# Two normalisations on VectorE, and batch 2's k turned ahead of its last two loads, in a fused windowed attention and MLP kernel

## The chip, the cores and the metric

The kernel runs on one core of one Trainium2 chip. A core has TensorE (PE: matmuls, with weight loads listed as PEld), VectorE (DVE), ScalarE (ACT), GpSimd (POOL) and SyncE (SP), each with its own in-order queue of instructions, and DMA queues that the engines feed. The metric is the device time of one execution in microseconds (us), the median over several runs. A profile, which lists every instruction of one further execution, explains it.

## The reference

Causal attention with a window of 64 keys over 8 batches, 8 heads, 576 positions and 64 columns per head; its output, as 4608 rows of 512, goes through two matrix products with h * cos(h) between them.

```python
scores = scale * np.matmul(q, k.transpose(0, 1, 3, 2))
rel = pos[:, None] - pos[None, :]
mask = (rel >= 0) & (rel < window)
scores = np.where(mask, scores, -1000000000.0)
attn = softmax(scores)                       # over the last axis
x = np.matmul(attn, v).transpose(0, 2, 1, 3).reshape(4608, 512)
h = x @ w_in                                 # 512 x 2048
out = (h * np.cos(h)) @ w_out                # 2048 x 512
```

## The kernel before, in words

**Units, groups, tiles.** Heads are taken in four pairs, and the 576 positions in nine blocks of 64, so a batch has 36 units (pair, block) of 128 partitions by 128 keys. A *group* is three or four units that go through the softmax together. The output rows are cut in nine M-tiles of 512 rows; M-tile `mt` covers eight blocks, so tile 1 holds the last block of batch 0 and blocks 0 to 6 of batch 1, tile 2 holds blocks 7 and 8 of batch 1 and blocks 0 to 5 of batch 2, and so on.

**The path of a group.** `g_scores` or `burst` multiplies q and k on TensorE (`s_ps`, L240 or L257). `g_max` adds the mask and takes the maximum on VectorE (`s`, `negm`, L273). `g_exp` takes exponentials and their sums on ScalarE (`e`, `den`, L284). `g_inv` inverts the sums on VectorE (`rden`, L291). `g_norm` multiplies e by rden into `w` on GpSimd (L298), unless it is given another engine. `g_trans` turns w: by TensorE into PSUM (`tw_ps`, L307) with a copy by `g_put` (L108) for the groups named in `direct`, otherwise by a DMA transpose from SP into `wT` (L310). `values` multiplies wT and v on TensorE (`o_ps`, L326), `put_x` copies that to `xT`, and the two products follow: `h_ps` (L347), sine on ScalarE (L489), product on VectorE (`gT`, L492), `out_ps` (L504), a copy to `out_sb` and a store.

**Where q and k come from.** Batches 0 and 1 are loaded whole and turned by TensorE. From batch 2 on `load_chunk` (L148, issued by GpSimd) brings q and k in five chunks of 128 positions each (the fifth has 64) into a row tile. Even and odd batches do not use different row tiles: batch 1 has `rows1`, all others share `rows0`. Slots 0 to 4 of the row tile hold the five q chunks and k's fifth chunk, slots 5 to 8 hold k's chunks 0 to 3. Two DMA transposes from SP (`turn`, L152) then make the turned tile `T`: `turn(b, 0, 5)`, called the q turn below, and `turn(b, 5, 9)`, the k turn. `load_v` (L158) brings v, also in five chunks from GpSimd, and `spread_v` copies its halves so that each block finds its 128 keys.

**The order.** The order on each engine is that of the program: tile 0 follows a list written out by hand (`FIRST`), and everything else is put on a plan with `at(time, function, ...)`. The matmul loops of an M-tile call `pump(time)`, which calls all planned steps up to that time in order of time. One M-tile takes `T = 32` units of planned time. The planned times only order the steps; the engines then run as their waits allow. A step that reads what a transfer writes waits for that transfer if the transfer was called earlier. If the reader is called first, the transfer waits for the reader.

**Before, around the change.** Batch 2's k chunks 0 to 3 are planned at 27.5, 28.4, 29.3 and 30.2, its k turn at 39.2 (7.2 into tile 1's time), behind all of them. Batch 3's k chunks are planned from 47 on. `g_norm` of batch 1's groups runs on GpSimd. The first of these groups is the last block of batch 0, the second is block 6 of batch 1. Tile 0's two stores are planned at 40 and 41, behind the k turn on SP.

**Resources that bind neighbours.** GpSimd's loads use eight completion counters in turn, so a load waits until the load eight places earlier has landed. Each SP transfer uses eight counters likewise. `w` has eight buffers, `e` six, `out_sb` three.

Of the kernel before, what the change touches and what calls it, by code (L numbers as in the profile page):

```python
# [33 lines left out]
T = 2 * Q  # L34
# [17 lines left out]
def kernel(  # L52
# [49 lines left out]
    def bank(which, name):  # L102
        if which == "t":
            return ps_t.tile([128, 512], F32, tag="t", name=name)
        return ps.tile([128, 512], F32, tag=which, name=name)

    def copy(engine, out, in_):
        {"a": nc.scalar.copy, "p": nc.gpsimd.tensor_copy}.get(engine, nc.vector.tensor_copy)(out, in_)  # L108
# [229 lines left out]
    def exp_table():  # L338
        nc.scalar.activation(small, small, AF.Exp, scale=0.0)
# [4 lines left out]
    def first(mt, ff, ks, start, stop):  # L344
        if start:
            st["h", ff] = bank((H_BANKS if mt else H_FIRST)[ff], "h_ps")
        nc.tensor.matmul(out=st["h", ff], lhsT=w_in_sb[:, ks, ff * 128:ff * 128 + 128],  # L347
                         rhs=st["xT", mt][:, ks], start=start, stop=stop)

    def skewed(mt, ks, n):  # L350
        for ff in range(SKEW):
            first(mt, ff, ks, n == 0, n == PAIRS - 1)

    def last_rows(gT, o_sb):
        ms = MT // 128 - 1
        for which, lo, hi in (("O1", 0, LAST), ("S", LAST, d_model)):
            o_ps = bank(which, "out_ps")[:, lo:hi]
            for ff in range(n_ff):
                nc.tensor.matmul(out=o_ps, lhsT=gT[ff // 2][:, ff % 2, ms * 128:ms * 128 + 128],  # L359
                                 rhs=w_out_sb[:, ff, lo:hi], start=ff == 0, stop=ff == n_ff - 1)  # L360
            to = moe.tile([128, MT], F32, tag="sin", name="last_sb", bufs=4)[:, lo:hi] if lo else o_sb[:, 1, lo:hi]
            copy("d" if lo else "a", to, o_ps)
            (nc.sync if lo else nc.scalar).dma_start(out=out[n_mt * MT - 128:n_mt * MT, lo:hi], in_=to)

    def store(o_sb, mt, ms0, e, n):
        r0 = mt * MT + (ms0 + e) * 128
        nc.sync.dma_start(out=out[r0:r0 + n * 128].rearrange("(a p) f -> p a f", p=128), in_=o_sb[:, e:e + n])
# [3 lines left out]
    def at(time, fn, *args):  # L371
        plan.append((time, len(plan), fn, args))

    def pump(time):
        plan.sort(key=lambda x: x[:2])
        while plan and plan[0][0] <= time:
            _, _, fn, args = plan.pop(0)
            fn(*args)
# [3 lines left out]
    n = n_first  # L382
    for t in range(B - 1):
        last = max(i for i, units in enumerate(groups) if units[0][0] == t + 1)
        time = T * t + Q - 1.4
        times = [time]
        for i in range(n, last + 1):
            times.append(times[-1] + PACE * len(groups[i]))
        if t:
            at(times[0], burst, n, BURSTS[0])  # L390
            at(times[4] + 0.1, burst, n + 4, BURSTS[1])
        else:
            for i in range(0, last + 1 - n, 2):
                at(times[max(i - 1, 0)] + (0.5 if i else 0), burst, n + i, (S_BANKS[i % 3], S_BANKS[(i + 1) % 3]))
        for i in range(last + 1 - n):
            time = times[i] + (0.3 if i > 3 and t else 0)
            lags = LAGS[:2] + tuple(T * t + T - 0.79 - time + 0.01 * s for s in range(3)) if n == last and t else LAGS
            for lag, fn in zip(lags, (g_max, g_exp, g_inv, g_norm)):
                at(time + lag, fn, n)
            at(time + (4.6 if n in direct else lags[-1]) if not t or i < 6 else T * t + T + 0.1 * i, g_trans, n)  # L400
            if n in direct:
                at(time + 4.9, g_put, n)
            ready.update({unit: time + (5.9 if n in direct else 8.5) for unit in groups[n]})
            n += 1
# [5 lines left out]
    for b in range(2, B):  # L410
        t0 = T * (b - 1)
        for c in range(NC):
            at(t0 - T + (4 + 0.5 * c if b == 2 else 5 + 0.9 * c), load_chunk, "q", b, c)
            at(t0 - T + ((27.5 if b == 2 else 15 if b == 3 else 10.5) + 0.9 * c if c < 4 else 6.5 if b == 2 else 9.6),
               load_chunk, "k", b, c)
            at(t0 + (0.5 if b == 2 else 14) + 0.8 * c, load_v, b, c)
        at(t0 - (4.1 if b == 2 else 5.6), turn, b, 0, 5)
        at(t0 + (7.2 if b == 2 else -5.5), turn, b, 5, 9)
        for half in range(2):
            at(t0 + 27.5 + half, spread_v, b, half, "d")  # L420
    for half in range(2):
        at(17.5, spread_v, 1, half, "dma")
    for mt in range(1, n_mt):
        for p in range(PAIRS):
            time = max(ready[b, p - p % 2 + i // TU, j] for i in range(2 * TU) for b, j in (divmod(mt * TU + i % TU, NU),))
            time = max(time, 25.5) if mt == 1 else T * mt - (8.01 if mt == n_mt - 1 else 1.01)
# [43 lines left out]
    for mt in range(n_mt):  # L470
        base = mt * T
        gT = []
        if mt:
            for ks in range(PAIRS):
                pump(max([base - 1] + [time for time, _, fn, args in plan
                                       if fn is put_x and args[:2] == (mt, ks)
                                       or mt == 1 and fn is values and args == (mt, ks + 1)]))
                skewed(mt, ks, ks)
        for ff in range(n_ff):
            for ks in range(PAIRS):  # L480
                if ff >= SKEW:
                    first(mt, ff, ks, ks == 0, ks == PAIRS - 1)
            h_ps = st.pop(("h", ff))
            sin = moe.tile([128, MT], F32, tag="sin", name="sin", bufs=4)
            if ff % 2 == 0:
                gt = moe.tile([128, 2, MT], BF16, tag="gT", name="gT", bufs=n_ff // 2 + 2)
                gT.append(gt)
            e = ff % 2
            nc.scalar.activation(sin, h_ps, AF.Sin, bias=math.pi / 2.0)  # L489
            if ff == n_ff - 1 and mt < B - 1:  # L490
                exp_table()
            nc.vector.tensor_tensor(out=gt[:, e], in0=h_ps, in1=sin, op=ALU.mult)  # L492
            pump(base + ff)
        half = n_ff // 2 if mt == 0 else n_ff
        for ms0 in range(0, MT // 128, 2):
            o_sb = moe.tile([128, 2, d_model], F32, tag="out", name="out_sb", bufs=3)
            o_ps = [bank(which, "out_ps") for which in (("O0",) if mt == n_mt - 1 and ms0 else ("O0", "O1"))]
            for step, (lo, e) in enumerate([(lo, e) for lo in range(0, n_ff, half) for e in range(2)]):
                ms = ms0 + e
                if mt == n_mt - 1 and ms == MT // 128 - 1:  # L500
                    last_rows(gT, o_sb)
                    break
                for ff in range(lo, lo + half):
                    nc.tensor.matmul(out=o_ps[e], lhsT=gT[ff // 2][:, ff % 2, ms * 128:ms * 128 + 128],  # L504
                                     rhs=w_out_sb[:, ff], start=ff == 0, stop=ff == n_ff - 1)
                    if ff % 4 == 3:
                        if ff == n_ff - 1:
                            copy("a" if e else "d", o_sb[:, e], o_ps[e])
                            if mt == n_mt - 1:
                                store(o_sb, mt, ms0, e, 1)  # L510
                        pump(base + Q + 4 * ms0 + step * half // 4 + ff % half // 4)
            if mt < n_mt - 1:
                at(base + T + (1.5 if mt else 8) + ms0 / 2, store, o_sb, mt, ms0, 0, 2)


# [28 lines left out]
```

## Time and profile before

| | us |
|---|---|
| median of 3 runs | 311.0 |
| lowest, highest | 310.4, 311.55 |
| profiled execution, its own time | 313.43 |
| its span, first to last instruction | 311.7 |

The span is what the profile's rows add up to; times in the rows count from its start. A row of the timeline gives the start, the duration, the engine, the line of the code, the operation with its output and input tiles, how many such instructions were merged, and in brackets how long the engine had been idle and who released it. Rows that end in DMA issues (`POOL ... DMA_DIRECT2D`, `SPq ...`) are the issuing only; when the data has landed is given apart. "PE s_ps <- DMA T" in brackets means that TensorE's matmul into `s_ps` stood until the transfer into `T` had landed. In the table by stages, the column after the engines is the granted TensorE clock (1.00 is full), then the DMA share and GB/s.

### The profile page before, as it was taken

What the parts mean: (1) busy time and instruction counts of PE and PEld (TensorE: products, weight loads), DVE (VectorE), ACT (ScalarE), POOL (GpSimd) and SP (SyncE); (2) the same over time, 40 slices, a digit from 0 to 9 for tenths busy, and PEclk for the clock granted to TensorE, in tenths of its full rate; (3) what the DMA queues carried; (4) which work ended last, traced back from release to release, by engine and by line L of the source; (5) the groups of instructions that cost most, each with busy time, mean ns of one, the idle gap of its engine ahead of it and who ended that gap; (6) DMA issues with size and microseconds to landing.
All of it is one profiled execution on the core that took longest, in us unless ns stands there. A gap on an engine that the chain in (4) does not pass through costs nothing.

```text
span 311.7 us, 7846 instructions
## 1 busy us (share of the span) xinstructions
PE 290.8 (93%) x2628; PEld 143.2 (46%) x2668; DVE 217.3 (70%) x831; ACT 236.2 (76%) x785; POOL 174.2 (56%) x202
## 2 busy tenths in 40 slices
PE   3769998898899999999999999999999999999995
PEld 2635444443345444544454445444544454454443
DVE  2875887668467887788778877887788878335701
ACT  4888689777798789978996999699969986116600
POOL 8996247894564976497649775967902630000000
PEclk9998999999799999999999999999999999999999
DMA  6999999899969999899999998999993342011011
GB/s 90 164 211 207 208 161 109 98 165 165 231 96 147 141 234 149 131 149 233 161 136 148 230 157 156 142 229 145 138 195 114 76 111 92 0 70 68 0 67 69
DMA packets 165577, 43.58 MB, mean 140 GB/s; under 512 B 154720, under 2 KB 161056, under 8 KB 165536
## 3 DMA queue, kind: packets, MB, share of 16 engines
q0 software_dynamic: 99632, 18.36, 74.9%
q1 hardware_dynamic: 65760, 24.52, 39.4%
q8 instruction: 21, 0.34, 0.4%
q10 hardware_dynamic: 144, 0.20, 0.2%
q14 instruction: 20, 0.16, 0.2%
HBM read 36.70 MB, written 9.44 MB: 148 GB/s over the span
## 4 chain that ended last, share of the span: by engine, by line
PE 76%; ACT 6%; DMA 6%; DVE 4%; POOL 4%; issue 3%; DVEq 0%; POOLq 0%; SPq 0%; ACTq 0%
PE h_ps L347 36%; PE out_ps L504 32%; ACT e L284 5%; DMA T<-rows 3%; PE o_ps L326 3%; PE s_ps L257 3%; DMA rows<-in_k_dram 2%; DVE s L273 2%; POOL w L298 1%; PE out_ps L359 1%; DMA rows<-in_q_dram 1%; DVE negm L269 1%; PE tw_ps L307 1%; POOL v L108 1%; POOL rows L148 1%
## 5 line engine op out<-in xcount | busy, mean ns | idle before, releaser
L347 PE MATMUL h_ps<-xT,w_in 128*128 128x512 bf16 x556 | 127.0, 381 | 2.2 <-DVE xT L108 0.6
L504 PE MATMUL out_ps<-w_out,gT 128*128 128x512 bf16 x543 | 124.5, 383 | 2.0 <-issue 1.3
L492 DVE TENSOR_TENSOR gT<-h_ps,sin 128x512 bf16<-128x512 f32 x144 | 95.6, 689 | 35.3 <-ACT sin L489 35.1
L489 ACT ACTIVATE sin<-h_ps 128x512 f32<-128x512 f32 x144 | 83.1, 599 | 34.2 <-PE h_ps L347 33.3
L284 ACT ACTIVATE e<-s,negm 128x128 f32<-128x128 f32 x256 | 98.7, 388 | 3.3 <-DVE negm L273 3.1
L298 POOL TENSOR_TENSOR w<-e,rden 128x512 bf16<-128x512 f32 (+1 forms) x78 | 77.1, 1001 | 39.1 <-DVE rden L291 35.2
L347 PEld LDWEIGHTS <-w_in 128*128 128x128 bf16 x576 | 56.1, 98 | 66.7 <-issue 1.8
L504 PEld LDWEIGHTS <-gT 128*128 128x128 bf16 x560 | 53.5, 98 | 63.7 <-issue 2.4
L273 DVE CUSTOM_DVE_ANT_0 s<-s_ps,mask 128x128 f32<-128x128 f32 x256 | 58.0, 284 | 2.2 <-PE s_ps L257 2.2
L284 ACT ACTIVATION_READ_ACCUMULATOR e<-s,negm 128x1 f32 x256 | 48.1, 188 | 0.0
L158 POOL DMA_DIRECT2D v<-in_v_dram x40 | 34.0, 876 | 11.0 <-PE out_ps L504 5.2
L148 POOL DMA_DIRECT2D rows<-in_q_dram x30 | 25.5, 872 | 22.1 <-DMA T<-rows 12.7
L108 ACT COPY out_sb<-out_ps 128x512 f32<-128x512 f32 (+1 forms) x18 | 10.2, 566 | 25.4 <-PE out_ps L504 19.9
L148 POOL DMA_DIRECT2D rows<-in_k_dram x30 | 25.7, 897 | 5.5 <-DMA T<-rows 5.5
L291 DVE RECIPROCAL rden<-den 128x4 f32<-128x4 f32 (+1 forms) x80 | 13.7, 172 | 16.6 <-ACT e L284 15.8
L108 DVE COPY out_sb<-out_ps 128x512 f32<-128x512 f32 x18 | 12.4, 689 | 17.0 <-PE out_ps L504 17.0
L108 DVE CAST xT<-o_ps 128x512 bf16<-128x512 f32 x27 | 17.5, 678 | 6.1 <-PE o_ps L326 5.8
L273 DVE DVE_READ_ACCUMULATOR2_ANT negm<- 128x1 f32 x256 | 21.2, 83 | 0.0
L257 PE MATMUL s_ps<-T 64*64 64x128 bf16 x512 | 11.8, 220 | 2.2 <-DMA T<-rows 2.2
L284 ACT ACTIVATE e<-s_ps,negm 128x128 f32<-128x128 f32 x32 | 11.4, 415 | 2.2 <-DVE negm L269 2.2
L257 PEld LDWEIGHTS <-T 64*64 64x64 bf16 x512 | 8.1, 106 | 10.4 <-issue 5.7
L326 PEld LDWEIGHTS <-v 128*64 128x64 bf16 x576 | 10.6, 112 | 4.7 <-issue 2.5
(50 smaller groups left out, 137.2 us busy)
## 6 DMA issues: line engine op xcount, KB each, us to landing
out_dram<-out_sb SPq DMA_DIRECT2D x16, 512.0 KB, 6.1
v<-in_v_dram POOLq DMA_DIRECT2D x32, 128.0 KB, 8.5
rows<-in_q_dram POOLq DMA_DIRECT2D x24, 128.0 KB, 5.8
rows<-in_k_dram POOLq DMA_DIRECT2D x24, 128.0 KB, 8.2
w_out<-in_moe_w_out_dram POOLq DMA_DIRECT2D x2, 1024.0 KB, 16.9
w_in<-in_moe_w_in_dram POOLq DMA_DIRECT2D x2, 768.0 KB, 12.7
wT<-w SPq DMA_TRANSPOSE x66, 3.7
out_dram<-out_sb SPq DMA_DIRECT2D x3, 256.0 KB, 2.0
```

The lines of the kernel that those rows point to most:

```text
L108: {"a": nc.scalar.copy, "p": nc.gpsimd.tensor_copy}.get(engine, nc.vector.tensor_copy)(out, in_)
L148: nc.gpsimd.dma_start(out=rows(b)[lo:lo + n, slot * 512:slot * 512 + 512].rearrange("p (h d) -> p h d", h=H), in_={"q": q, "k": k}[name][b ...
L158: nc.gpsimd.dma_start(out=vt.rearrange("p (h d) -> p h d", h=H), in_=v[b, :, c * 128:c * 128 + n, :].rearrange("h p d -> p h d"))
L257: nc.tensor.matmul(out=s_ps[cross][to, u].rearrange("p (a t) -> p a t", a=2), lhsT=q_cols(b, p, j)[d], rhs=k_cols(b, p, j)[d], start=True, ...
L273: nc.vector.tensor_tensor_reduce(out=s[:, u], in0=s_ps[:, u], in1=mask[:, 2 - j % 2 if j else 0], scale=-scale if b else -1.0, scalar=BIG, ...
L284: nc.scalar.activation(e[:, u], s[:, u], AF.Exp, bias=negm[:, u:u + 1], scale=1.0 if n < n_first else -1.0, accum_out=den[:, u:u + 1])
L298: (nc.gpsimd if engine == "p" else nc.vector).tensor_tensor(out=w[:, 0:u], in0=e[:, 0:u], op=ALU.mult, in1=rden[:, 0:u].unsqueeze(2).to_br ...
L326: nc.tensor.matmul(out=o_ps[64 * h:64 * h + 64, 64 * i:64 * i + 64], lhsT=vtiles[b % 3][:, max(j - 1, 0), 128 * p + 64 * h:128 * p + 64 * ...
L347: nc.tensor.matmul(out=st["h", ff], lhsT=w_in_sb[:, ks, ff * 128:ff * 128 + 128], rhs=st["xT", mt][:, ks], start=start, stop=stop)
L489: nc.scalar.activation(sin, h_ps, AF.Sin, bias=math.pi / 2.0)
L492: nc.vector.tensor_tensor(out=gt[:, e], in0=h_ps, in1=sin, op=ALU.mult)
L504: nc.tensor.matmul(out=o_ps[e], lhsT=gT[ff // 2][:, ff % 2, ms * 128:ms * 128 + 128], rhs=w_out_sb[:, ff], start=ff == 0, stop=ff == n_ff - 1)
```

## The change

```diff
-            for lag, fn in zip(lags, (g_max, g_exp, g_inv, g_norm)):
+            for lag, fn in zip(lags, (g_max, g_exp, g_inv)):
                 at(time + lag, fn, n)
+            if t or i > 1:
+                at(time + lags[3], g_norm, n)
+            else:
+                at(time + lags[2] + 0.01, g_norm, n, "d")
...
-            at(t0 - T + ((27.5 if b == 2 else 15 if b == 3 else 10.5) + 0.9 * c if c < 4 else 6.5 if b == 2 else 9.6),
-               load_chunk, "k", b, c)
+            at(t0 - T + ((19.4 if c < 2 else 28.6) + 0.01 * c if b == 2 else 10.5 + 0.9 * c) if c < 4 else
+               t0 - T + (6.5 if b == 2 else 9.6), load_chunk, "k", b, c)
...
-        at(t0 + (7.2 if b == 2 else -5.5), turn, b, 5, 9)
+        at(t0 - (4 if b == 2 else 5.5), turn, b, 5, 9)
...
-                at(base + T + (1.5 if mt else 8) + ms0 / 2, store, o_sb, mt, ms0, 0, 2)
+                at(base + T + (1.5 if mt else 3) + ms0 / 2, store, o_sb, mt, ms0, 0, 2)
```

The first two groups that follow tile 0's own (`t` is 0 and `i` is 0 or 1) are normalised by VectorE, directly behind their reciprocal. Batch 2's k chunks 0 and 1 are planned at 19.40 and 19.41, chunks 2 and 3 at 28.62 and 28.63. Batch 2's k turn is planned at 28, directly behind its q turn, which stays at 27.9. Batch 3's k chunks are planned 4.5 earlier, from 42.5. Tile 0's two stores are planned at 35 and 36.

The k turn of batch 2 is thereby called before the loads of chunks 2 and 3. For these two chunks it turns what the row tile then holds, which is a part of batch 0's rows, and the scores of batch 2 against those keys are made of that; the two loads wait for the turn.

The order on the engines that follows from the planned times:

```
GpSimd   before: ... k c4 | w w | w x7 | k c0  k c1 | w | k c2 | w | k c3 | w | v x5 | q(3) x5 | k(3) x5 ...
         after:  ... k c4 | k c0  k c1 | w x8 | k c2  k c3 | w w | v x5 | q(3) x5 | k(3) x5 ...
SP       before: ... wT x4 | q turn | wT wT | k turn | store store | wT x6 ...
         after:  ... wT x4 | q turn | k turn | wT wT | store store | wT x6 ...
VectorE  before: ... s x8 | rden | s x6 | rden | wT copy ...
         after:  ... s x8 | rden  w | s x6 | rden  w | wT copy ...
```

`(3)` marks batch 3's loads; the other loads are batch 2's. The orders on TensorE and ScalarE are unchanged, and nothing else moves on any queue.

## The prediction

> **What bounds the kernel now.** The page's first lines come first, then the chain of waits in order of time.
>
> ```profile
> span 311.7 us, 7846 instructions
> PE 290.8 (93%) x2628; PEld 143.2 (46%) x2668; DVE 217.3 (70%) x831; ACT 236.2 (76%) x785; POOL 174.2 (56%) x202
> ...
> 62.91 6.10 DMA rows<-in_k_dram
> 69.14 9.78 DMA T<-rows
> ...
> 79.05 0.64 PE s_ps L257 x32
> ```
>
> TensorE is busy for 93% of the span, so time is won where it stands still. The longest transfers on the chain after the start are batch 2's: a k chunk lands at 69.0, the turn of k waits for it and lands at 78.9, and batch 2's first burst of scores waits for the turn. The timeline of TensorE shows what that costs (first column start, second duration, in brackets the idle time before):
>
> ```profile
> 48.28 0.40 PE L307 MATMUL tw_ps<-ident,w 128*128 128x128 bf16 x4 [0.76 <-POOL w L298]
> ...
> 61.07 0.34 PE L307 MATMUL tw_ps<-ident,w 128*128 128x128 bf16 x3 [1.03 <-POOL w L298]
> ...
> 63.48 13.34 PE L347 MATMUL h_ps<-xT,w_in 128*128 128x512 bf16 x60
> 79.05 0.64 PE L257 MATMUL s_ps<-T 64*64 64x128 bf16 x32 [2.23 <-DMA T<-rows]
> ...
> 96.02 1.44 PE L326 MATMUL o_ps<-wT,v 128*64 128x64 bf16 x64
> ```
>
> TensorE is through with tile 1's first product at 76.82 and stands 2.23 us. A second loss follows, which only the table by stages shows (columns: stage, its length, busy time of PE, PEld, DVE, ACT, POOL, then the granted clock):
>
> ```profile
> 76.45:79.86 3.41, 1.18 (x35) 0.63 (x35) 1.75 (x5) 2.22 (x4) 0.41 (x1) 1.00 1.92 229
> 79.86:83.27 3.41, 3.19 (x9) 1.21 (x9) 2.49 (x23) 3.38 (x17) 3.41 (x5) 0.50 1.69 255
> ```
>
> After a stage with 1.18 us of work the granted clock is 0.50 for 3.41 us: half of it, 1.7 us, is lost. So the late turn costs 2.2 + 1.7 = 3.9 us, and batch 2's values start at 96.02. A later tile does the same stretch undisturbed:
>
> ```profile
> 111.38 0.64 PE L257 MATMUL s_ps<-T 64*64 64x128 bf16 x32
> ...
> 126.90 1.41 PE L326 MATMUL o_ps<-wT,v 128*64 128x64 bf16 x64
> ```
>
> From burst to values it takes 126.90 - 111.38 = 15.5 us there, against 17.0 here.
>
> **The change, part by part.** *The first two normalisations.* POOL loses two w and VectorE gains two:
>
> ```profile
> L298 DVE TENSOR_TENSOR w<-e,rden x2: 679/949/1219, 14.9 to 23.0; 128x512 bf16<-128x512 f32 x2
> ...
> 43.95:58.82 14.87, 14.46 (x73) 1.00 1.02 105
> ```
>
> VectorE does such a w in 0.68 to 1.22 us. The first one removes the 0.76 us for which TensorE waits at 48.28 (POOL was issuing loads). The second row is ScalarE alone over the exponentials: 14.46 busy of 14.87, so they can move up by 0.41 at most. I put this part at 0.4, bounded by 0.8 gained (the whole wait) and by 1.6 lost (two w of 1.22 in VectorE's queue, less the 0.8).
>
> *Loads and turn of batch 2's k.* On POOL, chunks 0 and 1 now stand where the two w stood, long before anyone asks for them: nothing. Chunks 2 and 3 come after the ninth group's w, as one pair. The turn of k comes directly behind the turn of q on SP's queue, ahead of the loads of chunks 2 and 3. It waits for chunks 0 and 1 alone, and the other two chunks wait until it has read the tile. What stands behind them on POOL waits too. POOL and SP as they are (SPq rows are issues):
>
> ```profile
> 57.66 1.83 POOL L148 DMA_DIRECT2D rows<-in_k_dram  x2
> ...
> 61.92 1.05 POOL L298 TENSOR_TENSOR w<-e,rden 128x512 bf16<-128x512 f32 x1
> 62.91 0.94 POOL L148 DMA_DIRECT2D rows<-in_k_dram  x1
> ...
> 64.86 4.25 POOL L158 DMA_DIRECT2D v<-in_v_dram  x5
> 69.06 4.24 POOL L148 DMA_DIRECT2D rows<-in_q_dram  x5
> 73.21 0.78 POOL L148 DMA_DIRECT2D rows<-in_k_dram  x1
> 79.45 3.51 POOL L148 DMA_DIRECT2D rows<-in_k_dram  x4 [5.46 <-DMA T<-rows]
> 82.94 1.08 POOL L298 TENSOR_TENSOR w<-e,rden 128x512 bf16<-128x512 f32 x1
> ...
> 91.77 1.04 POOL L298 TENSOR_TENSOR w<-e,rden 128x512 bf16<-128x512 f32 x1 [1.08 <-DMA wT<-w]
> ```
>
> ```profile
> 59.24 4.41 SPq L152 DMA_TRANSPOSE T<-rows  x1
> 63.71 3.50 SPq L310 DMA_TRANSPOSE wT<-w  x2
> 69.14 4.33 SPq L152 DMA_TRANSPOSE T<-rows  x1
> 73.57 1.04 SPq L367 DMA_DIRECT2D out_dram<-out_sb  x2
> ```
>
> When does the pair of turns land? A later batch has such a pair with no loads beside it (first line of each: issue time of min/median/max, then its start; second: time to landing):
>
> ```profile
> L152 SPq DMA_TRANSPOSE T<-rows x1: 3282/3282/3282, 94.3 to 94.3; - x1
> ...
> DMA to landing us min/median/max: 6.6/6.6/6.6
> ...
> L152 SPq DMA_TRANSPOSE T<-rows x1: 3066/3066/3066, 97.8 to 97.8; - x1
> ...
> DMA to landing us min/median/max: 5.1/5.1/5.1
> ```
>
> The second lands 97.8 + 5.1 - 94.3 = 8.6 after the first starts. The first will start at about 58.9 (59.24, less a little of the 0.4 above), with POOL's loads silent since they wait for it, so k's turn lands at 67.5. The other bound is the pace of the row at 69.14, which the chain shows landing 9.78 after its start: 58.9 + 4.4 + 9.8 = 73.1. I take 67.5, as the quiet pair is the nearer case. The burst at some 76.4 (76.82 - 0.4) no longer waits in either: the 3.9 us go.
>
> What is late instead is POOL. After the landing it needs 0.5 us to go on (a later batch: issue at 101.44 below, the q turn landed at 100.9), so chunk 2 goes out at 68.0, where before it went at 60.97. From there it issues two loads (1.9 by the 0.94 row), two w (2.1), five v (4.25), five q (4.24), one k (0.78) and four k (3.51), 16.8 in all, up to 84.8. Then there is the depth of its queue: each load waits for the one eight places earlier, and a later batch shows the wait.
>
> ```profile
> 101.44 4.26 POOL L148 DMA_DIRECT2D rows<-in_q_dram  x5 [2.86 <-DMA T<-rows]
> ...
> 114.84 0.69 POOL L158 DMA_DIRECT2D v<-in_v_dram  x1 [1.45 <-DMA rows<-in_k_dram]
> ...
> rows<-in_q_dram POOLq DMA_DIRECT2D x4, 128.0 KB, 8.3
> ```
>
> There (first two rows) a series of 15 loads beside two stores loses 1.45 us; here it is 17 beside two stores. I take 1.45, bounded by 0 and 2.9 (twice). So POOL is free for batch 2's w at 86.2, 3.3 us later than the 82.94 of before, while TensorE's burst is 2.6 us earlier.
>
> Who waits for that? The values of tile 2 need six of these w, each turned through SP. The last pair in the trace:
>
> ```profile
> L310 SPq DMA_TRANSPOSE wT<-w x1: 1189/1189/1189, 92.8 to 92.8; - x1
> ...
> DMA to landing us min/median/max: 2.5/2.5/2.5
> ```
>
> First w done at 86.2 + 1.05 = 87.25; six issues at 1.2, the sixth from 93.25; landed at 95.75, the fifth at 94.55. TensorE comes to the values at 76.4 + 15.5 = 91.9, stands 2.6 us for the fifth (the first two pairs of heads need it), and again for the sixth; the second half of the values takes 0.72, so they end at 96.5. Before they ended at 97.46: 1.0 gained. But a stand of 2.6 us is longer than the 2.23 that halved the clock, so I charge 1.7 again. Sum: -1.0 + 1.7 = +0.7.
>
> [...]
>
> *The rest.* Batch 3's k loads get earlier times but keep their places on POOL, and the first tile's stores keep theirs on SP, behind the two wT: nothing by themselves. Through those wT the stores follow POOL's new wait; issued at about 73.4 as against 73.57, they meet the same loads. The late wT belong to tile 2's values, 20 us away. Batch 3's turns start behind the sixth wT, at 94.5 as against 94.3, and the tiles from there on are as they were.
>
> The sum stands on the profiled execution: 311.7 + 0.7 = 312.4 of span. That execution took 313.43 us with its ends, the runs shown a median of 311.0 (310.4 to 311.55); the same 0.7 gives 311.7 for the median.
>
> **The rivals.** [...]
>
> *POOL is in time.* No wait for the queue's depth: POOL free at 84.8, values end at 95.1, 2.4 gained, the stand at 1.2 and too short for the clock: 308.6. For it: chunks 0 and 1 and the turns no longer load the queues. Against: the 1.45 above. At the very best no w is late and all of 3.9 + 0.4 is won: 306.7.
>
> *The queue fills (slower).* Batch 3's q loads, issued from 69.06 on beside a turn and the stores, took a median of 8.3 to land (last row of the fence before); if loads now take 9.5, the ninth to last load (issued at 77) frees the last one only at 86.5, and POOL is free at 87.4. Values end at 97.7, 0.2 late, and the clock is charged: +1.9, 312.9. It decides from 0.9 us beyond my 1.45. For it: two more loads than in the later batch. Against: no turn runs beside them now.
>
> *The pair of turns stays slow.* If the turn that takes 9.8 us does so without the loads beside it, k lands at 73.1, and POOL and the values are 5.6 later than in my sum: 311.7 + 5.6 = 317.3. Little speaks for it.
>
> *The change doesn't do what it says*, that is, the burst waits on: this would need a landing after 76.4, 13 us after the issue, which no row of T shows; left out.
>
> **How the numbers follow.** The forecast, waits that change places with +0.7, has 0.40; the clock holds 0.17; POOL in time 0.20; the queue fills 0.18; slow turns 0.05. Half a per cent, 1.55 us, is about what a measurement of this kernel can tell from no change. Faster than 309.45: the third case and a little of the second, 0.22. Slower than 312.55: the last two and a part of the forecast's spread, 0.29. The rest, 0.49, is within. The range reaches from the case of POOL in time to just beyond the filled queue: 308.4 to 313.8; the forecast alone runs from 310.6 to 312.6.
>
> **What would show it.** T's landing for k at 67 to 68, and no stand before batch 2's burst, shows the first step. POOL's k chunk 2 waiting on T for some 7 us, its first w of batch 2 at about 86, and a stand of 2 to 3 us before o_ps at about 92, released by wT or w, show the second; a 0.50 stage behind it the third. First w of batch 2 before 84, or values that start without a stand, would make the prediction wrong towards faster; a load waiting on loads for more than 2.4 us, towards slower.

## The result, and the profile after

The changed kernel took a median of 314.04 us (312.85 to 315.78, 20 runs) beside 311.81 us for the kernel before (310.36 to 316.16, 20 runs on the same chip). The ratio is 1.007, 95% interval 1.0043 to 1.0098: slower by 0.7%, 2.2 us. The forecast was 311.7, no change, with a range up to 313.8. Ratios and their intervals leave out the runs that lie over 1.5% above the fastest run of the same kernel, so a ratio can differ from the quotient of two medians, which are of all runs.

The two profiled executions, however, are alike to 0.01 us: 313.44 us with a span of 311.7 after, 313.43 us with a span of 311.7 before. That is the riddle of this case. First what the profile after shows, beginning with TensorE's waits from 40 to 100 us (columns: line waited for, total us, times, longest):

```profile
PE o_ps L326 <- DMA wT<-w: 1.6, 2, 0.9
PE o_ps L326 <- DVE v L108: 1.4, 1, 1.4
```

The wait of the burst for T is gone, and a wait of the values has come. The timeline of TensorE gives the places (start, duration, instruction, idle time before it):

```profile
46.88 0.40 PE L307 MATMUL tw_ps<-ident,w 128*128 128x128 bf16 x4
...
75.93 0.64 PE L257 MATMUL s_ps<-T 64*64 64x128 bf16 x32
...
91.45 0.32 PE L326 MATMUL o_ps<-wT,v 128*64 128x64 bf16 x8
93.17 0.25 PE L326 MATMUL o_ps<-wT,v 128*64 128x64 bf16 x4 [1.40 <-DVE v L108]
94.36 0.69 PE L326 MATMUL o_ps<-wT,v 128*64 128x64 bf16 x32 [0.94 <-DMA wT<-w]
95.72 0.75 PE L326 MATMUL o_ps<-wT,v 128*64 128x64 bf16 x20 [0.68 <-DMA wT<-w]
96.40 15.10 PE L347 MATMUL h_ps<-xT,w_in 128*128 128x512 bf16 x64
111.44 0.64 PE L257 MATMUL s_ps<-T 64*64 64x128 bf16 x32
```

The w that TensorE waited for before, until 48.28, now holds it no more: the same transposes are at 46.88, without a wait. The burst starts at 75.93 without a wait, 3.1 us earlier than before. The values start at 91.45, 4.6 us earlier, stand three times, 3.0 us in all, and end at 96.4, 1.0 us earlier. At the next burst nothing is left of it: 111.44 against 111.38. The table by stages says where that 1.0 us went (stage, length, busy PE, PEld, DVE, ACT, POOL, then the granted clock):

```profile
91.87:95.28 3.41, 0.95 (x36) 0.75 (x37) 2.05 (x4) 1.47 (x6) 2.71 (x3) 1.00 0.56 111
95.28:98.69 3.41, 2.96 (x26) 1.49 (x26) 1.43 (x4) 1.49 (x2) 0.82 (x1) 0.50 1.05 130
```

The stand leaves 0.95 us of work in 3.41, and the next 3.41 us run at half clock, as they did behind the burst before. Of these 3.41 us, 2.3 lie behind the end of the values, and the first product takes 15.10 us in place of 13.97: 1.1 is lost. GpSimd's timeline shows why the values stand:

```profile
59.37 0.82 POOL L298 TENSOR_TENSOR w<-e,rden 128x384 bf16<-128x384 f32 x1 [2.47 <-PE o_ps L326]
67.28 1.83 POOL L148 DMA_DIRECT2D rows<-in_k_dram  x2 [7.08 <-DMA T<-rows]
69.10 2.06 POOL L298 TENSOR_TENSOR w<-e,rden 128x512 bf16<-128x512 f32 x2
71.08 4.26 POOL L158 DMA_DIRECT2D v<-in_v_dram  x5
75.29 4.24 POOL L148 DMA_DIRECT2D rows<-in_q_dram  x5
80.90 2.56 POOL L148 DMA_DIRECT2D rows<-in_k_dram  x3 [1.37 <-DMA v<-in_v_dram]
83.81 1.75 POOL L148 DMA_DIRECT2D rows<-in_k_dram  x2 [0.35 <-DMA rows<-in_q_dram]
85.57 9.01 POOL L298 TENSOR_TENSOR w<-e,rden 128x512 bf16<-128x512 f32 x9
```

The loads of k's chunks 2 and 3 hold GpSimd for 7.08 us until the k turn has landed; everything behind them is late, the queue's depth adds 1.37 + 0.35, and batch 2's w, which went out from 82.94 on as they became ready, start at 85.57 and run end to end.

### The profile page after: what moved, and what is told of

Read it like the earlier page. It is cut to its first block, busy times and chain, and to the rows that moved or that the text cites. A ratio compares the mean times of both kernels' runs of the same rounds, so it can differ in the third digit from the quotient of the medians.

```text
span 311.7 us, 7881 instructions
## 1 busy us (share of the span) xinstructions
PE 295.8 (95%) x2668; PEld 143.9 (46%) x2668; DVE 221.1 (71%) x833; ACT 235.5 (76%) x785; POOL 171.9 (55%) x200
## 4 chain that ended last, share of the span: by engine, by line
PE 80%; DVE 5%; POOL 5%; DMA 5%; ACT 2%; issue 2%; POOLq 0%; DVEq 0%
PE h_ps L347 38%; PE out_ps L508 32%; DMA rows<-in_q_dram 4%; POOL w L298 3%; PE o_ps L326 3%; PE s_ps L257 3%; POOL v L158 1%; PE out_ps L359 1%; DVE s L273 1%; DVE negm L269 1%; PE tk_ps L182 1%; DVE w L298 1%; PE tq_ps L182 1%; DMA wT<-w 1%; PE s_ps L240 1%
## 5 line engine op out<-in xcount | busy, mean ns | idle before, releaser
L347 PE MATMUL h_ps<-xT,w_in 128*128 128x512 bf16 x576 | 129.3, 383 | 0.9 <-ACT xT L108 0.5
L298 POOL TENSOR_TENSOR w<-e,rden 128x512 bf16<-128x512 f32 (+1 forms) x76 | 74.3, 994 | 35.1 <-DVE rden L291 31.0
L284 ACT ACTIVATION_READ_ACCUMULATOR e<-s,negm 128x1 f32 x256 | 48.9, 191 | 0.0
L326 PE MATMUL o_ps<-wT,v 128*64 128x64 bf16 x576 | 13.1, 200 | 3.0 <-DMA wT<-w 1.6
L108 DVE COPY v<-v 64x1536 bf16<-64x1536 bf16 (+1 forms) x13 | 12.5, 963 | 0.2
```

Of the source, the lines that this page charges most:

```text
L284: nc.scalar.activation(e[:, u], s[:, u], AF.Exp, bias=negm[:, u:u + 1], scale=1.0 if n < n_first else -1.0, accum_out=den[:, u:u + 1])
L298: (nc.gpsimd if engine == "p" else nc.vector).tensor_tensor(out=w[:, 0:u], in0=e[:, 0:u], op=ALU.mult, in1=rden[:, 0:u].unsqueeze(2).to_br ...
L326: nc.tensor.matmul(out=o_ps[64 * h:64 * h + 64, 64 * i:64 * i + 64], lhsT=vtiles[b % 3][:, max(j - 1, 0), 128 * p + 64 * h:128 * p + 64 * ...
```

## The experiments

Two questions were open. Is the loss the queue behind the two waiting loads (queue theory), or VectorE's new work (VectorE theory)? And what makes the medians differ when the profiles don't (clock theory)? The order of the planned times alone decides; so the parts of the change that leave every queue's order as it was, the stores' times and batch 3's k loads, give the same instructions as before and were not run apart. Every ratio below is to the kernel before on the same chip; it had a median of 312.35 us in 35 runs beside the first four kernels, and 311.92 in 23 beside the last three.

### All loads ahead of the turns

```diff
-            at(t0 - T + ((19.4 if c < 2 else 28.6) + 0.01 * c if b == 2 else 10.5 + 0.9 * c) if c < 4 else
+            at(t0 - T + ((19.4 if c < 2 else 27.5) + 0.01 * c if b == 2 else 10.5 + 0.9 * c) if c < 4 else
```

Here all four chunks of batch 2's k are loaded before they are turned.

> The changed kernel, with batch 2's k chunks 2 and 3 loaded ahead of both turns, behind the eighth group's w on GpSimd; the k turn then waits for all four chunks, and no load waits for it. Queue theory (the time goes where GpSimd's queue stands 7 us behind the k turn, so that batch 2's w are late for tile 2's values): k lands at 68 to 69, GpSimd is free for batch 2's w at 75 to 78, no stand of TensorE before batch 2's burst and none before tile 2's values, no half clock there; the values start at about 91.5 and the profile's span is 307 to 308, 4 us under both kernels; the time some 3 us under the kernel before. VectorE theory (the loss comes from the two w that VectorE took over, or from its v copies beside GpSimd's w): the values still wait 1.4 us for the v copies and the time stays above the kernel before.

309.02 us (308.27 to 309.8, 12 runs), ratio 0.9898, 0.9867 to 0.9929. GpSimd's timeline first:

```profile
56.43 1.83 POOL L148 DMA_DIRECT2D rows<-in_k_dram  x2
...
77.17 0.88 POOL L148 DMA_DIRECT2D rows<-in_k_dram  x1 [1.95 <-DMA rows<-in_q_dram]
79.64 1.03 POOL L298 TENSOR_TENSOR w<-e,rden 128x512 bf16<-128x512 f32 x1 [1.59 <-DVE rden L291]
```

Then TensorE's:

```profile
75.52 0.64 PE L257 MATMUL s_ps<-T 64*64 64x128 bf16 x32
...
91.03 1.71 PE L326 MATMUL o_ps<-wT,v 128*64 128x64 bf16 x64
...
106.59 0.64 PE L257 MATMUL s_ps<-T 64*64 64x128 bf16 x32
```

The last two chunks go out at 56.43. GpSimd is through with its loads at 78.05 and waits for VectorE, not the other way round. Neither the burst nor the values wait, and the next burst is at 106.59, 4.9 us before that of the changed kernel. The span is 306.8, a little under the 307 to 308 expected; this execution had no half clock in tile 0 either (its mean clock is 1.000). The k turn, issued at 62.6, landed only 7.7 to 8.0 later, at about 70.5 and not at 68 to 69, but still ahead of the burst. The queue theory holds, and this kernel beats both.

### VectorE's part alone

```diff
-            for lag, fn in zip(lags, (g_max, g_exp, g_inv, g_norm)):
+            for lag, fn in zip(lags, (g_max, g_exp, g_inv)):
                 at(time + lag, fn, n)
+            if t or i > 1:
+                at(time + lags[3], g_norm, n)
+            else:
+                at(time + lags[2] + 0.01, g_norm, n, "d")
```

This goes into the kernel before.

> The kernel before, with only the two normalisations on VectorE. Queue theory: TensorE's 0.76 us stand at 48.3 goes and everything behind it moves by 0.4 to 0.8, the k turn too, since its last load follows GpSimd's w; the stand of about 2.2 us before batch 2's burst stays, and the time is 0 to 0.8 us under the kernel before. VectorE theory: the time is 1 to 2 us above it.

310.83 us (309.92 to 314.64, 12 runs), ratio 0.9978, 0.9937 to 1.0019. The loss of 1 to 2 us that the VectorE theory asks for is outside the interval; a gain of 0 to 0.8 fits it, but isn't told from none. Its profile keeps the stand at the burst:

```profile
78.53 0.64 PE L257 MATMUL s_ps<-T 64*64 64x128 bf16 x32 [2.49 <-DMA T<-rows]
```

### Loads and turn alone

The same lines the other way: the changed kernel with `g_norm` on GpSimd again.

> The changed kernel, with the two normalisations back on GpSimd: loads, turn and stores as in the changed kernel. Chunks 2 and 3 of batch 2's k are still turned from what the row tile holds. Queue theory: the loss stays, 2 to 3 us above the kernel before, with the stand before tile 2's values. VectorE theory: the loss goes, within 0.5 us of the kernel before or under it.

314.41 us (313.36 to 315.96, 12 runs), ratio 1.008, 1.0044 to 1.0115. The whole loss is in the loads and the turn. TensorE's timeline shows the same stands about 1 us later, and the table by stages shows half clock behind them for twice as long, 6.83 us:

```profile
94.14 0.25 PE L326 MATMUL o_ps<-wT,v 128*64 128x64 bf16 x4 [1.38 <-DVE v L108]
95.30 1.06 PE L326 MATMUL o_ps<-wT,v 128*64 128x64 bf16 x32 [0.92 <-DMA wT<-w]
96.68 0.75 PE L326 MATMUL o_ps<-wT,v 128*64 128x64 bf16 x20 [0.31 <-DMA wT<-w]
...
94.99:101.82 6.83, 6.21 (x63) 3.19 (x63) 2.06 (x4) 1.87 (x2) 1.61 (x3) 0.50 0.93 153
```

The wait for VectorE's v copies is there although VectorE has none of the new work, so it does not come from the two w on VectorE.

### The two loads behind v

```diff
-            at(t0 - T + ((19.4 if c < 2 else 28.6) + 0.01 * c if b == 2 else 10.5 + 0.9 * c) if c < 4 else
+            at(t0 - T + ((19.4 if c < 2 else 36.6) + 0.01 * c if b == 2 else 10.5 + 0.9 * c) if c < 4 else
```

> The changed kernel, with the loads of batch 2's k chunks 2 and 3 behind batch 2's w and v on GpSimd, not ahead of them; the k turn stands where the change put it and takes the same stale chunks. Queue theory (it is what stands behind the waiting loads that costs): w goes on at 60 and v at 62, the two loads find k landed at about 67 and wait at most 1 us, GpSimd is free for batch 2's w at 77 to 80, no stand before the values; the time is that of all loads first, 309, within 0.5 us. Rival (the place of the turn itself, or the traffic beside it, costs): the time stays above 312.

309.28 us (308.82 to 310.26, 6 runs), ratio 0.989, 0.9834 to 0.9945. GpSimd's timeline, and TensorE's at the values:

```profile
59.73 2.89 POOL L298 TENSOR_TENSOR w<-e,rden 128x384 bf16<-128x384 f32 x3 [2.47 <-PE o_ps L326]
62.57 4.26 POOL L158 DMA_DIRECT2D v<-in_v_dram  x5
70.60 1.75 POOL L148 DMA_DIRECT2D rows<-in_k_dram  x2 [3.77 <-DMA T<-rows]
...
80.73 1.07 POOL L298 TENSOR_TENSOR w<-e,rden 128x512 bf16<-128x512 f32 x1
...
91.81 1.67 PE L326 MATMUL o_ps<-wT,v 128*64 128x64 bf16 x64
```

The loads still wait, 3.77 us and not the 1 at most that was expected, since the turn, now beside v's loads, lands later: they go out at 70.60, in the changed kernel at 67.28. But two w and five loads are out before, GpSimd is free at 80.73, 4.8 us earlier than in the changed kernel, and TensorE's waits for the values are gone. So the turn's early place and its stale chunks cost nothing that these runs tell; what cost was the work queued behind the two loads.

### All loads ahead, normalisation on GpSimd

The first experiment's edit, with `g_norm` as in the kernel before.

> All four loads of batch 2's k ahead of both turns, with the two normalisations back on GpSimd. Queue theory: still no stand at the burst nor at the values; the stand of 0.76 us at 48.3 is back, so the time is 0.4 to 0.8 above that of all loads first, 309.5 to 309.8. VectorE theory: the time is under that of all loads first.

309.82 us (309.27 to 310.58, 12 runs), ratio 0.9916, 0.9883 to 0.9948. That is 0.8 us over the 309.02 with VectorE's part. The two ratios' intervals overlap, so the part is only indicated by the times; the traces agree with its sign. TensorE's stand at 48 is back, 0.95 us long, and the burst is at 76.64 here and at 75.52 there.

### Filling the stands

The clock theory was tried by work that nobody reads, put into the stand. In the changed kernel before tile 2's values:

```diff
+    def fill(n):
+        f = bank("X0", "fill_ps")
+        for _ in range(n):
+            nc.tensor.matmul(out=f, lhsT=w_in_sb[:, 0, 0:128], rhs=w_in_sb[:, 1, 0:512], start=True, stop=True)
...
+            if mt == 2 and p == 0:
+                at(time, fill, 6)
             at(time, values, mt, p)
```

> The changed kernel, with six matmuls of 128x512 that nobody reads just before tile 2's values, 1.3 us of TensorE work in a stand of 3.0. Clock theory (the stand before the values always halves the clock for 3.4 us, while the shorter stand of the kernel before halves it in a part of its runs only): the half clock behind the values goes, the mean clock rises from 0.989 to 0.995, and the time falls by 1 to 1.7 us, to about 0.5 us above the kernel before. Rival (the clock is the same in both kernels' runs, the loss is all waiting): the time stays where the changed kernel is, or rises by up to 1 us.

312.75 us (312.25 to 314.64, 12 runs), ratio 1.004, 1.0008 to 1.0073: its median is 1.3 us under that of the changed kernel, by work added to it. The two ratios' intervals overlap, but the runs of this kernel speak for themselves: four with a mean clock of 0.982 to 0.988 took 314.13 to 314.64 us, the eight others, at 0.993 to 1.000, took 312.25 to 312.99. The same function in the kernel before, ahead of batch 2's burst:

```diff
+            if t == 1:
+                at(times[0], fill, 5)
             at(times[0], burst, n, BURSTS[0])
```

> The kernel before, with five matmuls of 128x512 that nobody reads just before batch 2's first burst, 1.1 us of TensorE work in a stand of 2.2. Clock theory (in about a third of the runs of the kernel before the stand at the burst halves the clock, and its profile was one of these): runs with a mean clock under 0.99 fall from 13 of 35 to 2 of 12 or fewer, the median falls to about 311, and a profile without the half clock starts tile 2's values at 94 to 94.5 instead of 96.02. Rival (the spread of the kernel before is in the transfers, not in the clock): the share of such runs and the median of 312.3 stay.

311.33 us (310.17 to 315.49, 12 runs), ratio 0.9963, 0.9928 to 0.9998. The interval only just leaves 1 out. Its profile had no half clock behind the burst, and so comes nearest to an execution of the kernel before without that stage (three rows of the timeline, two of the table by stages):

```profile
79.49 0.64 PE L257 MATMUL s_ps<-T 64*64 64x128 bf16 x32 [1.52 <-DMA T<-rows]
...
94.77 1.44 PE L326 MATMUL o_ps<-wT,v 128*64 128x64 bf16 x64
...
110.14 0.64 PE L257 MATMUL s_ps<-T 64*64 64x128 bf16 x32
...
76.70:79.50 2.80, 1.28 (x9) 0.43 (x7) 1.38 (x2) 2.08 (x3) 0.00 (x0) 1.00 2.15 197
79.50:83.00 3.50, 3.50 (x46) 1.85 (x47) 2.69 (x24) 2.67 (x14) 3.11 (x4) 1.00 1.45 287
```

Although its turn lands 0.4 later than before, its values start at 94.77 as against 96.02 (94 to 94.5 had been expected), and the next burst is 1.2 us earlier. The mean granted clock of every run tells the rest. In a run of some 310 us a stage of 3.41 us at half clock takes 0.0055 off the mean (half of 3.41, over 310). The profiles of the kernel before and of the changed kernel, both at 0.989, have two such stages each: one in tile 0 (21.84 to 25.25 before, 20.19 to 23.60 after) and one behind the stand at the burst or at the values. By this estimate 0.994 is one stage and 0.989 two. The mean doesn't say where they lie. The profile of VectorE's part alone is at 0.984, by the estimate three; one is behind the burst, where 24 matmuls took 7.04 us beside 5.35 in the first experiment, and the other two are not placed. Three of the 23 runs of the kernel before that are under 0.99 took only 310.4 to 310.6 us, so their stages may lie elsewhere than at the burst. Of the 35 others, five took over 313 us; their one stage may lie at the burst. So the counts are right to a few runs. (The expectation above counted 13 in the first 35 runs; it is 14.)

| kernel | runs under 0.99 | median of these, us | median of the others, us |
|---|---|---|---|
| before (both batches) | 23 of 58 | 313.84 | 311.36 |
| changed | 19 of 20 | 314.12 | 312.85 (one run) |
| before, filled | 1 of 12 | 315.49 (one run) | 311.32 |
| changed, filled | 4 of 12 | 314.15 | 312.45 |
| VectorE's part alone | 5 of 12 | 313.13 | 310.71 |
| loads and turn alone | 12 of 12 | 314.4 | - |
| all loads ahead | 0 of 12 | - | 309.02 |
| all loads ahead, normalisation on GpSimd | 1 of 12 | 309.27 (one run) | 309.9 |
| two loads behind v | 0 of 6 | - | 309.28 |

The kernel before is under 0.99 in 23 of 58 runs, the changed kernel in 19 of 20. Where both have it their medians differ by 0.3 us (by 0.5 without the runs over 315 us, seven and three), and the two profiles by 0.01. The changed kernel's filled runs that escape it are 1.1 us over the escaped runs of the kernel before, so that much is not the clock. The fill does not always help. In the profile of the filled changed kernel the stage at half clock follows a stage with 1.58 of 3.41 us busy:

```profile
92.84:96.25 3.41, 1.58 (x51) 1.04 (x51) 2.46 (x4) 1.34 (x3) 2.09 (x4) 1.00 0.42 84
96.26:99.67 3.41, 3.41 (x27) 1.51 (x27) 1.29 (x2) 0.96 (x1) 0.50 (x1) 0.50 1.19 183
```

## Why the prediction was wrong

*The waits were right, step by step.* Turn of k landed: forecast 67.5, measured 66.7, from this view of T's transfer (issue, start; then time to landing):

```profile
L152 SPq DMA_TRANSPOSE T<-rows x1: 3154/3154/3154, 61.5 to 61.5; - x1
...
DMA to landing us min/median/max: 5.2/5.2/5.2
```

Chunk 2 out: 68.0, measured 67.28. Wait for the queue's depth: 1.45, measured 1.72. GpSimd free for batch 2's w: 86.2, measured 85.57. Values reached: 91.9, measured 91.45. Values ended: 96.5, measured 96.4. Half clock behind them: charged, and there, but it cost 1.1 and not 1.7, since the first part of it lay on the values themselves and their stands. VectorE's part was put too small: 0.4, at most 0.8, while TensorE was through with tile 1's first product by 75.93 in place of 76.82, 0.9 earlier. That changed nothing for the values, which waited for GpSimd.

*The step that failed is the last one,* "the same 0.7 gives 311.7 for the median". The sum of +0.7 took two clock terms against each other: 1.7 won back at the burst, 1.7 lost at the values. The first was read from the profile as if every run had it. The profiled execution had it, as did about 23 in 58 runs; by its mean clock the median run of the kernel before had nothing to win back there. Between the two profiled executions the change is 0.0, and +0.7 less the 0.6 by which the half clock behind the values was charged too high gives about that. That 313.43 + 0.7 = 314.1 meets the changed kernel's median of 314.04 is partly luck. Taken against a run without the stage, the 1.7 that the -1.0 counts as won at the burst isn't there to win: -1.0 + 1.7 for that, + 1.7 for the values, is +2.4, or +1.8 with the 1.1 that was measured. The medians differ by 2.2, and those of the runs with the stage after and without it before by 2.8 (314.12 and 311.36). So the stage explains most of the difference; 0.4 to 1.0 us of it stays open. A part may be half clock that lasts two stages, as in the profile of loads and turn alone: five of the changed kernel's 20 runs have a mean of 0.984 or less.

The base was off as well. The 311.0 to which the 0.7 was added was the median of three runs; 20 runs gave 311.81. That is 0.8 of the 2.3 us by which the time was missed.

The sign was there to see. The profiled execution's 313.43 us lay 1.9 above the highest of the runs shown, 311.55. The prediction named both numbers and carried the 0.7 from one to the other without asking about the gap. A run's time stands 1.7 to 1.9 us over its span in every run with both, so the median run's span was about 309.3, 2.4 less than the profile's. That gap is about one half-clock stage (1.7) and a little more.

*The rivals.* "The clock holds", 0.17, is the case of 310.0 in which no half clock follows the new stand. That a stand of 2.6 us can leave the clock whole was the author's estimate, and no profile shows it; by the mean clocks it came in 1 run of 20. The same chance was not asked for the old stand, where by the mean clocks it came in about 35 runs of 58. "POOL in time" is what the better orders do; that its stand of 1.2 us is too short for the clock was an estimate too, and the profiles show full clock behind stands of 0.76 and 1.03 us in the kernel before and of 1.52 in the filled one, but half clock behind two of 1.18 and 0.61 us in tile 0 of the kernel before (19.64 and 21.81). "The queue fills" came by a part only: 1.72 us of waits for depth, under its 2.35. A stand before the values by VectorE's v copies, 1.40 us, was foreseen by no case; it did not set the end, since the sixth wT landed later anyway.

## What to carry to other kernels

Before a sum is built on a profile, set the profiled execution's time against the runs; if it lies outside them, ask which stage of it the other runs lack, and do not count what only that execution lost as something to win. A transfer that is told to wait, here a load whose target is still being read, belongs behind whatever on its queue can go at once: moving two loads behind seven instructions took the ratio to the kernel before from 1.007 to 0.989. Both of these kernels turn two chunks of k before they are loaded, so their scores for batch 2 are not those of the reference; loading all four chunks ahead of the turns is as fast, 0.9898, and leaves nothing out. And several short stands of TensorE in a row can cost more than their sum, here 3.0 us of stands and 1.1 us by the half clock behind them, so it may pay to put work of any kind into them: the filled changed kernel took 312.75 us beside 314.04, with intervals of the ratios that overlap.

## What the runs showed of the hardware

Half clock was granted for 3.41 us at a time in the profiles of the two kernels, and for 6.83 us in that of loads and turn alone. The 3.41 us ahead of it had 1.60 us of TensorE work (18.42 to 21.84) and 1.18 (76.45 to 79.86) in the kernel before, 1.94 (16.77 to 20.19) and 0.95 (91.87 to 95.28) in the changed one, and 1.58 in the filled changed one. The work in such a stage doesn't settle it: behind 1.91 us (15.01 to 18.42, before) the clock stayed at 1.00. Nor does the length of one stand: at the burst a stand of 2.23 us had half clock behind it, at the values stands of 1.40, 0.94 and 0.68 us in a row, and no stand at either place was longer than 2.49 us (VectorE's part alone). So no limit for either follows from these profiles, and the 1.7 us that the prediction charges for a stand stays an estimate: half of 3.41 us, if TensorE has work for all of them.

VectorE's second v copy (64x2048 bf16) took 1.86 us in the changed kernel, where GpSimd's nine w run end to end, and 0.69 in the first experiment, where GpSimd pauses between them. The two rows, from VectorE's timelines of the changed kernel and of the first experiment:

```profile
91.25 1.86 DVE L108 COPY v<-v 64x2048 bf16<-64x2048 bf16 x1
```

```profile
90.65 0.69 DVE L108 COPY v<-v 64x2048 bf16<-64x2048 bf16 x1
```

It was 1.86 in the kernel with loads and turn alone too, where the nine w run end to end as well, from 86.53 for 9.01 us, and 0.69 in the kernel before. Whether the w make the copy longer is not shown: no run changed one of them alone.
